# Moving table work between engines and overlapping the stages ahead of an attention loop

## The chip, the cores and the metric

The kernel runs on one NeuronCore of a Trainium2 chip. The metric is the device time of one execution in microseconds (us). A profile of one execution is used beside it; its span runs from the first to the last instruction of the program. TensorE does matmuls, VectorE and GpSimd elementwise work, ScalarE functions and copies, and DMA queues are fed by SP (SyncE), ScalarE and GpSimd.

## What is computed

Two independent halves are laid side by side in the output, [2048, 576 + 576].

```python
# A: sliding-window attention, 32 heads of 18 channels, window 256
qkv = x @ wqkv                                  # x [2048, 576]
p = softmax(where(0 <= i - j < 256, q @ k.T * 18 ** -0.5, -1e9))
a = (p @ v) @ wo
# B: diagonal state-space model, 576 channels, 128 states
dt = exp(log_dt)
P[d, n, l] = exp(dt[d] * (A_re + 1j * A_im)[d, n] * l)      # l = 0..2047
K[d, l] = real(sum_n C[d, n] * P[d, n, l] * dt[d] * B[d, n])
y = causal_convolution(u, K) + u * Dskip        # in the reference by an FFT over 4096
```

## The kernel before, in words

**Order of the work.** Everything up to the attention is written with pools of tiles and left to a scheduler, which fixes each engine's order when the kernel is built, from the order in which operations are emitted (`merge` interleaves several generators by weight) and its own estimates. From `attention` on the order is the written one (`manual_schedule`). Engines run their queues strictly in order. A pool gives a tile of a name one of a few buffers; a new tile waits until the old one's readers are done. Pools are stacked: memory of a closed pool is reused by pools opened later, whose first use waits for it.

**Projections (`proj`, L182 to L252).** x and the weights are scaled by a power of two from their largest absolute value (`amax`, L161; across partitions on GpSimd, L144) and split into a high and a low half-precision part: `wh`, `wl` (L209, L210), `xh`, `xl` (L226 to L229). So x is read twice: once in 8 slices of 256 columns for its maximum (L188 to L195), once for the split. Projections are 14 matmuls each (`mm14`, L172); their results are split again (L236, L237) and stored to DRAM as `qd` and `vd`.

**Tables (`s4_prep`, `tables`).** K is built from tables of exponentials and sines in 36 steps of 16 channels (`n = 2 * NQ`; two steps share one group q of 32). Angles come from small outer products on TensorE into PSUM (`outer`, L314, pool `xps`, two buffers). `fraction` (L318) rounds them on ScalarE (L324), subtracts on VectorE (L325) and takes the absolute value on ScalarE (L326). `exps_ab` and `exps_q` (L334, L344) are exponentials, for four steps at a time. `factors` (L348 to L371) takes two sines and then six operations on VectorE (L358, L364, L365, L367, L368, L369) to make `A` and `tr`. `products` (L380) multiplies these out on GpSimd into two tiles of a pool `P` with two buffers; `qtable` makes the other operand `Q` (sines L395, L396 into PSUM; L400 to L403 on VectorE); `taps` (L418) contracts both on TensorE, 64 matmuls a step, and every second step copies the result into the tile K (L424). ScalarE loads a new function table (ACT_TABLE_LOAD) whenever exponentials and sines alternate.

**First transform (`s1`, L454).** The convolution is a two-step transform. The first step is a matmul with `w1` (L461), an eviction (`evac`, L125: three of four on ScalarE, L128, the fourth on VectorE, L130) and a store to DRAM (`gx` for u, `gk` for K). For u it runs in 16 pieces beside the tables (`s1_u`); for K (`s1_k`) in 8 pieces of 1152 columns, after all pools of projections and tables are closed.

**Attention (`attention`).** `att_setup` clears the tiles for Q and K on VectorE (L596 to L599). Per unit (four heads, half of the sequence; 16 units) `load_unit` reads Q, K, V; `gmax` finds row maxima (matmul L636, VectorE L643) and writes them as a row into Q by a DMA; `scores` (L677, exponential L679, masks on GpSimd L688) and `values` (L700) follow in 96 items. The convolution's second step and inverse (`conv`, L480: L500, L508, L526 to L537) is cut into parts that are dealt to the items; six parts run beside `gmax(0)` before the first item. The output projection (L903) comes last.

The way in which the pools of the stages follow each other is this (`build`):

```python
with ExitStack() as ek:
    self.pool(ek, "K", 1)
    with ExitStack() as e1:
        ...
        with ExitStack() as e2:
            self.pool(e2, "prep", 1)
            self.s4_prep()
        for n, b in (("wq", 1), ("raw", 2), ("x", 1), ...):
            self.pool(e1, n, b)
        ...
        merge((proj, 56), (tables, 400), (s1u, 12))
    with ExitStack() as e1:
        ...                       # s1_k
with ExitStack() as e1:
    ...                           # attention
```

Of the kernel before, what the change touches and what calls it, by code (L numbers as in the profile page):

```python
# [102 lines left out]
class Kernel:  # L103
# [17 lines left out]
    def pool(self, es, name, bufs, space=None):  # L121
        kw = {} if space is None else {"space": space}
        self.p[name] = es.enter_context(self.tc.tile_pool(name=name, bufs=bufs, **kw))
# [37 lines left out]
    def amax(self, out, v):  # L161
        self.nc.vector.tensor_reduce(out, v, axis=AX.XY, op=OP.max, apply_absolute_value=True)
# [19 lines left out]
    def proj(self):  # L182
# [3 lines left out]
        amx = sp.tile([128, 12], F32, name="amx")  # L186
        wr = self.p["K"].tile([128, 5, 1728], F32, name="K")
        for c in range(8):  # L188
            t = self.p["raw"].tile([128, 5, 256], F32, name="raw")
            self.load_rows(t, a["xT"], slice(c * 256, c * 256 + 256))  # L190
            self.amax(amx[:, c:c + 1], t)
            if c % 2 == 0:
                cs = slice(c // 2 * 432, c // 2 * 432 + 432)
                self.load_rows(wr[:, :, cs], a["wqkv"], cs)
            yield  # L195
        for c in range(4):
            self.amax(amx[:, 8 + c:9 + c], wr[:, :, c * 432:c * 432 + 432])
            yield
        px, self.sx = self.pow2_scale(amx[:, 0:8], "x")
        pw, self.sw = self.pow2_scale(amx[:, 8:12], "w")  # L200
# [117 lines left out]
    def fraction(self, x, pool, n, w):  # L318
# [7 lines left out]
        nc.scalar.activation(ab, f, AF.Abs)  # L326
        return f, ab

    def exps_ab(self, s):

        for q in (2 * s, 2 * s + 1):
            x = self.outer(self.al, q, [self.mul["c_ca"]], 0, GC)
            m = self.p["mab"].tile([128, GC, 12], F32, name="mab")
            self.nc.scalar.activation(m, x.rearrange("p (c m) -> p c m", m=12), AF.Exp)  # L334
# [3 lines left out]
    def exps_q(self, s):  # L338

        for c in range(4 * s, 4 * s + 4):  # L340
            mg = self.p["mg"].tile([128, HC, 64], F32, name="mg")
            for e in range(2):
                x = self.outer(self.al, c // 2, [self.mul["c_cm"]], c % 2 * HC + e * 8, 8)
                self.nc.scalar.activation(mg[:, e * 8:e * 8 + 8], x.rearrange("p (c m) -> p c m", m=64), AF.Exp)  # L344
                yield
            self.mg[c] = mg

    def factors(self, q):  # L348

        nc, tt, pool = self.nc, self.nc.vector.tensor_tensor, self.p["ab"]  # L350
# [5 lines left out]
        nc.scalar.activation(tr[:, :, 1, :], v(f), AF.Sin, scale=TWO_PI)  # L356
        nc.scalar.activation(tr[:, :, 0, :], v(ab), AF.Sin, scale=-TWO_PI, bias=self.halfpi)
# [11 lines left out]
        nc.vector.scalar_tensor_tensor(A[:, :, 0:4], t2[:, :, 0], -1.0, t1[:, :, 1], op0=OP.mult, op1=OP.subtract)  # L369
# [19 lines left out]
    def qtable(self, c):  # L389
# [5 lines left out]
        nc.scalar.activation(sn, v(f), AF.Sin, scale=-TWO_PI)  # L395
# [627 lines left out]
```

## Time and profile before

| | us |
|---|---|
| median of 3 runs | 1079.5 (1076.2 to 1081.78) |
| the profiled execution | 1075.61 |
| its span | 1073.6 |

The profile's views are told where they are used. Rows of groups give the line, engine, operation, output and input tiles with their shapes, the count, then busy time in us and the mean of one in ns, then the engine's idle time just before them and who ended it. "PE" is TensorE's matmuls, "PEld" its weight loads, "DVE" VectorE, "ACT" ScalarE, "POOL" GpSimd, "SPq" SP's queue of DMAs. PEclk is the share of TensorE's full clock that was granted. A row of waits reads: engine and line that waited, who released it, us in total, times, longest. Busy time of TensorE contains stalls inside its pipeline.

### The profile page before, as it was taken

What the parts mean: (1) busy time and instruction counts of PE and PEld (TensorE: products, weight loads), DVE (VectorE), ACT (ScalarE), POOL (GpSimd) and SP (SyncE); (2) the same over time, 40 slices, a digit from 0 to 9 for tenths busy, and PEclk for the clock granted to TensorE, in tenths of its full rate; (3) what the DMA queues carried; (4) which work ended last, traced back from release to release, by engine and by line L of the source; (5) the groups of instructions that cost most, each with busy time, mean ns of one, the idle gap of its engine ahead of it and who ended that gap; (6) DMA issues with size and microseconds to landing.
All of it is one profiled execution on the core that took longest, in us unless ns stands there. A gap on an engine that the chain in (4) does not pass through costs nothing.

```text
span 1073.6 us, 26801 instructions
## 1 busy us (share of the span) xinstructions
PE 857.8 (80%) x10332; PEld 450.7 (42%) x10332; DVE 736.2 (69%) x1859; ACT 619.9 (58%) x955; POOL 511.1 (48%) x606
## 2 busy tenths in 40 slices
PE   1535879897988797987578888878888899988787
PEld 0313436554744464553234333333333344434345
DVE  2879685669576845226676788888878766767564
ACT  1776758776797784233146655566566656644471
POOL 0004344435452632010235677766876666666770
PEclk9966989998998998999889999999999999999999
DMA  9665423442344232588616456454645644579763
GB/s 271 168 184 160 105 53 88 109 94 59 85 111 96 55 74 64 130 217 239 188 49 180 138 147 175 147 148 127 176 113 177 185 118 142 146 185 256 204 190 121
DMA packets 155911, 152.27 MB, mean 142 GB/s; under 512 B 36856, under 2 KB 134392, under 8 KB 155592
## 3 DMA queue, kind: packets, MB, share of 16 engines
q1 hardware_dynamic: 148152, 131.98, 45.3%
q0 software_dynamic: 6128, 14.60, 5.4%
q10 hardware_dynamic: 1504, 3.99, 1.3%
q8 instruction: 81, 1.33, 0.6%
q14 instruction: 46, 0.38, 0.1%
HBM read 89.12 MB, written 61.01 MB: 140 GB/s over the span
## 4 chain that ended last, share of the span: by engine, by line
PE 37%; DVE 25%; ACT 10%; DMA 10%; issue 9%; POOL 5%; SPq 2%; DVEq 0%; ACTq 0%; POOLq 0%
PE pp L172 8%; PE r L636 4%; PE po L700 4%; PE r L903 4%; PE r L500 4%; PE kp L418 4%; PE pp L461 3%; DVE jk L643 3%; POOL P L688 2%; DMA gk<-g 2%; PE ST L677 2%; PE x L314 2%; PE r L508 2%; DVE tr L358 2%; ACT P L679 2%
## 5 line engine op out<-in xcount | busy, mean ns | idle before, releaser
L643 DVE CUSTOM_DVE_ANT_0 jk<-r,bias 128x288 f32<-128x288 f32 (+7 forms) x512 | 198.0, 433 | 88.7 <-PE r L636 88.0
L679 ACT ACTIVATE P<-ST,esc 128x1024 f32<-128x1024 f32 (+1 forms) x192 | 202.0, 1059 | 92.9 <-PE ST L677 92.1
L380 POOL TENSOR_TENSOR m<-A,tr 128x1024 f32<-128x1024 f32 x72 | 149.5, 2098 | 194.2 <-PE kp L418 139.1
L688 POOL TENSOR_SCALAR_AFFINE_SELECT P<-P 128x512 f32<-128x512 f32 x240 | 171.7, 745 | 103.2 <-ACT P L679 100.8
L636 PE MATMUL r<-K,qb 128*64 128x288 f16 (+7 forms) x1024 | 130.5, 297 | 36.7 <-DVE qb L627 10.7
L700 PE MATMUL po<-P,V 128*32 128x256 f32 (+2 forms) x1408 | 100.2, 395 | 17.5 <-POOL P L688 8.1
L418 PE MATMUL kp<-Q,m 128*32 128x64 f32 x4608 | 88.3, 230 | 27.6 <-DVE Q L401 10.0
L636 PEld LDWEIGHTS <-qb 128*64 128x64 f16 x1024 | 60.3, 109 | 119.3 <-issue 65.6
L536 POOL TENSOR_TENSOR Y<-t,t 64x288 f32<-64x288 f32 x64 | 53.5, 835 | 109.8 <-DVE t L531 107.8
L418 PEld LDWEIGHTS kp<-Q,m 128*32 128x32 f32 x4608 | 75.2, 116 | 56.3 <-issue 41.7
L461 PE MATMUL pp<-ut,w 128*128 128x288 f32 x128 | 52.8, 538 | 40.9 <-DMA ut<-in_u_dram 18.6
L677 PE MATMUL ST<-Q,K 64*128 64x384 f16 (+2 forms) x704 | 73.5, 280 | 3.0 <-DMA Q<-mt 2.9
L237 DVE SCALAR_TENSOR_TENSOR qst<-pp,qst 128x512 f16<-128x512 f32 x36 | 24.7, 685 | 64.7 <-ACT qst L236 61.8
L128 ACT ACTIVATE g<-pp 128x288 f32<-128x288 f32 (+1 forms) x84 | 34.5, 447 | 40.4 <-DMA gk<-g 22.0
L700 PEld LDWEIGHTS po<-P,V 128*32 128x32 f32 x1408 | 35.7, 110 | 52.5 <-issue 25.7
L537 POOL TENSOR_TENSOR Y<-t,t 64x288 f32<-64x288 f32 x64 | 54.5, 852 | 3.8
L461 PEld LDWEIGHTS pp<-ut,w 128*128 128x128 f32 x128 | 28.9, 245 | 61.1 <-issue 24.1
L326 ACT ACTIVATE ab<-k 128x512 f32<-128x512 f32 (+1 forms) x54 | 31.9, 590 | 37.0 <-DVE k L325 36.6
L172 PE MATMUL pp<-xh,wh 128*128 128x512 f16 x180 | 47.9, 388 | 1.2 <-DVE xh L229 1.2
L172 PEld LDWEIGHTS <-wh 128*128 128x128 f16 x324 | 32.0, 101 | 39.3 <-issue 6.6
L172 PE MATMUL pp<-xh,wl 128*128 128x512 f16 x180 | 48.3, 392 | 0.0
L500 PE MATMUL r<-tx,w 128*64 128x288 f32 x256 | 40.2, 430 | 9.9 <-DMA tx<-gx 8.7
(177 smaller groups left out, 1756.1 us busy)
## 6 DMA issues: line engine op xcount, KB each, us to landing
gx<-g SPq DMA_DIRECT2D x32, 288.0 KB
qd<-qst SPq DMA_DIRECT2D x72, 128.0 KB
gk<-g SPq DMA_DIRECT2D x16, 576.0 KB
tx<-gx SPq DMA_DIRECT2D x16, 576.0 KB
tk<-gk SPq DMA_DIRECT2D x16, 576.0 KB
h<-ho SPq DMA_DIRECT2D x16, 576.0 KB
raw<-in_xT_dram SPq DMA_DIRECT2D x16, 512.0 KB
Q<-qd SPq DMA_DIRECT2D x32, 216.0 KB
```

The source lines that it names most:

```text
L172: self.nc.tensor.matmul(ps, u, v, start=(i == 0), stop=(i == len(ops) - 1))
L380: self.nc.gpsimd.tensor_tensor(m, A[:, ch, a0:a0 + 8].unsqueeze(3).to_broadcast(sh), tr[:, ch, part, 0:8].unsqueeze(2).to_broadcast(sh), o ...
L418: nc.tensor.matmul(kp[32 * st:32 * st + 32, c % 2 * JJ2 + j, :], m[:, ch, a0:a0 + 32], Q[:, ch, term % 2, :], start=(term == 0), stop=(ter ...
L461: nc.tensor.matmul(ps, self.w1[:, part, :], src[:, o:o + k], start=True, stop=True)
L500: nc.tensor.matmul(ps[64 * par:64 * par + 64], w2[:, par, 64 * part:64 * part + 64], t[:, 2 * hs:2 * hs + 2, par, :], start=True, stop=True)
L537: nc.gpsimd.tensor_tensor(Y[par][64:128], t1[sl, 1], t2[sl, 1], op=OP.add)
L636: nc.tensor.matmul(ps[64 * b:64 * b + 64, :n], self.qb[:, b, t, :], d["K"][:, b, k0:k0 + n], start=True, stop=True, skip_group_check=True)
L643: nc.vector.tensor_tensor_reduce(out=jk[:, :n], in0=ps[:, :n], in1=self.bias[:, 288 - n:], scale=1.0, scalar=-3e38, op0=OP.add, op1=OP.max ...
L677: nc.tensor.matmul(ps[:, u, o:o + n], d["K"][h, jp, k0:k0 + 128], d["Q"][h, jp, q0:q0 + n], start=True, stop=True, skip_group_check=True)
L679: nc.scalar.activation(pt[:, 2 * jp:2 * jp + 2, lo:hi], ps[:, :, lo:hi], AF.Exp, scale=self.esc)
L688: nc.gpsimd.affine_select(v, v, pattern=[[0, 4], [sg, 128]], compare_op=OP.is_ge, fill=0.0, base=-1 if far else 0, channel_multiplier=-sg)
L700: nc.tensor.matmul(self.po[32 * j:32 * j + 32, t0 * 128:t1 * 128], V[:, kb * 76 + 19 * j:kb * 76 + 19 * j + 32], pt[:, j, o:o + (t1 - t0) ...
```

## The change

1. **x is read first.** `proj` reads x once, contiguously, in five pieces into the buffers that later hold `wh`, `wl` and one `qst`, takes its maxima, and then reads the weights; its first step is emitted ahead of `s4_prep`. x is still read a second time for the split.
2. **Two-sided pools.** Pools get a side of the memory and finer waits for reuse: projections, K, the first transform and their loads lie on the right, tables and then the attention on the left. So buffers for x don't wait for `prep`, and attention's tiles not for the projections' pools.
3. **Absolute values masked.** The sign bit is cleared on VectorE instead of the absolute value on ScalarE.
4. **Table factors on GpSimd.** The six operations of `factors` move from VectorE to GpSimd (the last becomes a multiplication of `A[8:12]` by -1). `products(c + 1)` is emitted after `taps(c - 1)`.
5. **Ordered functions.** Exponentials and sines go through `act`, which makes the scheduler keep their written order on ScalarE. By the built order ScalarE loads a table 19 times instead of 37.
6. **K's transform.** 16 pieces of 576 columns instead of 8 of 1152, with the PSUM buffers of the projections; ten run after the tables, six beside `gmax(0)`, where six parts of the convolution ran. Those are dealt to the items (101 parts instead of 95 over the same 76 items). The weights of `merge` now let tables, projections and u's transform end together.

```diff
     def pool(self, es, name, bufs, space=None, side="left"):
         kw = {} if space is None else {"space": space}
+        if space != DRAM:
+            kw.update(side=side, reuse_waits="tile")
...
-        for c in range(8):
-            t = self.p["raw"].tile([128, 5, 256], F32, name="raw")
-            self.load_rows(t, a["xT"], slice(c * 256, c * 256 + 256))
-            self.amax(amx[:, c:c + 1], t)
...
+        flat = a["xT"].rearrange("r c -> (r c)").rearrange("(p n) -> p n", p=128)
+        for i, nm in enumerate(("wh", "wl")):
+            t = wp.tile([128, 4320], F32, name=nm)
+            for c in range(2):
+                o = 2160 * (2 * i + c)
+                nc.sync.dma_start(t[:, 2160 * c:2160 * c + 2160], flat[:, o:o + 2160])
+                self.amax(amx[:, 2 * i + c:2 * i + c + 1], t[:, 2160 * c:2160 * c + 2160])
+        t = self.p["pst"].tile([128, 576], F32, name="qst")
+        nc.sync.dma_start(t, flat[:, 8640:])
+        self.amax(amx[:, 4:5], t)
         for c in range(4):
-            self.amax(amx[:, 8 + c:9 + c], wr[:, :, c * 432:c * 432 + 432])
-            yield
+            cs = slice(c * 432, c * 432 + 432)
+            self.load_rows(wr[:, :, cs], a["wqkv"], cs)
+            self.amax(amx[:, 5 + c:6 + c], wr[:, :, cs])
+        yield
...
-        nc.scalar.activation(ab, f, AF.Abs)
+        nc.vector.tensor_scalar(ab.bitcast(I32), k, 0x7FFFFFFF, None, op0=OP.bitwise_and)
         return f, ab
+
+    def act(self, *args, **kw):
+
+        self.tc.stamp_issue_order_token(self.nc.scalar.activation(*args, **kw).ins, "transcendentals")
...
     def factors(self, q):
 
-        nc, tt, pool = self.nc, self.nc.vector.tensor_tensor, self.p["ab"]
+        nc, tt, pool = self.nc, self.nc.gpsimd.tensor_tensor, self.p["ab"]
...
-        nc.vector.scalar_tensor_tensor(A[:, :, 0:4], t2[:, :, 0], -1.0, t1[:, :, 1], op0=OP.mult, op1=OP.subtract)
+        nc.gpsimd.tensor_scalar(A[:, :, 0:4], A[:, :, 8:12], -1.0, None, op0=OP.mult)
...
             if c + 1 < n:
-                self.products(c + 1)
                 self.phases(c + 1)
                 yield
...
             if c:
                 yield from self.taps(c - 1)
+            if c + 1 < n:
+                self.products(c + 1)
...
-        for b in range(8):
-            self.s1(kf[:, b * 1152:(b + 1) * 1152], self.gk, 8 * b, 8, "s1p")
+        for b in range(16):
+            self.s1(kf[:, b * 576:(b + 1) * 576], self.gk, 4 * b, 4, pp[0])
...
-                k = share(n - 2, 95, 76) if n < 78 else share(n - 78, 16, 17) if n < 95 else 0
+                k = share(n - 2, 101, 76) if n < 78 else share(n - 78, 16, 17) if n < 95 else 0
...
+            self.pool(ek, "K", 1, side="right")
+            self.pool(ek, "s1s", 2, side="right")
+            self.pool(ek, "pps", 3, PSUM, side="right")
...
+                for n, b in (("s1u", 2), ("wq", 1), ("raw", 2), ("x", 1), ("pst", 2)):
+                    self.pool(e1, n, b, side="right")
...
+                next(proj)
                 with ExitStack() as e2:
                     self.pool(e2, "prep", 1)
                     self.s4_prep()
...
+                merge((part(proj, 4), 4), (part(tables, 16), 16), (part(s1u, 2), 2))
+                merge((proj, 56), (tables, 308), (s1u, 14))
+                for _ in part(s1k, 10):
+                    pass
...
+                self.attention_start()
+                merge((self.gmax(0), 19), (s1k, 6))
+                self.begin(1)
+                ek.close()
```

`attention_start` loads units 0 and 1, as the head of `attention` did. The exponential tables get four buffers (`mab`) instead of three.

More of the change, by code (lines that the diff above doesn't have):

```diff
@@ L515, in conv @@
         nx = load(0)
+        yield
         last = None
@@ L780, in attention @@
             self.begin(n)
+            if n == 0:
+                next(conv)
             streams = []
@@ L980, in build @@
                 nc.sync.dma_start(self.dsk, a["dsk"].partition_broadcast(128))
[L981 to L987 removed]
+                self.attention(self.conv())
+            e0.close()
 def kernel(**inputs):
```

83 lines of the change are left out of this document (35 added, 48 removed).

## The prediction

> **What bounds the kernel now.** I read the page's head first, then the busy time by stage, then what TensorE waits for in the longest stage.
>
> ```profile
> span 1073.6 us, 26801 instructions
> PE 857.8 (80%) x10332; PEld 450.7 (42%) x10332; DVE 736.2 (69%) x1859; ACT 619.9 (58%) x955; POOL 511.1 (48%) x606
> ```
> ```profile
> core 0: us, PE busy (x) PEld busy (x) DVE busy (x) ACT busy (x) POOL busy (x), PEclk, DMA share, GB/s
> 0.00:101.60 101.60, 38.91 (x321) 21.22 (x322) 69.81 (x79) 56.98 (x71) 11.23 (x13) 0.82 0.70 199
> 101.60:421.00 319.40, 269.75 (x5281) 165.47 (x5280) 221.95 (x328) 237.52 (x405) 141.09 (x68) 0.93 0.36 85
> 421.00:466.00 45.00, 44.90 (x251) 25.57 (x249) 7.12 (x11) 10.28 (x22) 1.45 (x4) 1.00 0.59 129
> 466.00:513.00 47.00, 35.69 (x97) 17.63 (x96) 26.73 (x26) 16.20 (x36) 3.51 (x1) 0.96 0.84 240
> 513.00:543.50 30.50, 16.09 (x109) 7.76 (x110) 20.29 (x80) 5.44 (x11) 6.93 (x10) 0.81 0.50 147
> 543.50:1073.60 530.10, 452.50 (x4278) 213.02 (x4277) 390.31 (x1336) 293.52 (x412) 346.89 (x510) 0.98 0.56 158
> ```
>
> The stretches are mine. Up to 101.6 us no projection runs: inputs land, maxima are taken. From 101.6 to 421 projections (L172) and tables (L418) share TensorE; to 466 the rest of the projections runs alone; to 513 the transform of the kernel K (L461 on K) runs alone, with the DMA at 0.84 of its time; to 543.5 the first maxima (L636, L643) and six parts of the convolution; then attention, 530.1 us, which the change hardly touches. So the change has 543.5 us to work on. In the mixed stretch TensorE is busy 269.75 of 319.4 us, at a granted clock of 0.93 against 1.00 where projections run alone. What it waits for there:
>
> ```profile
> PE x L314 <- DVE k L325: 19.3, 5, 6.1
> PE pp L461 <- DVE qst L237: 9.1, 2, 4.9
> PE kp L418 <- ACT K L424: 5.1, 6, 1.4
> PE kp L418 <- POOL m L380: 4.3, 3, 2.5
> PE kp L418 <- DVE Q L401: 4.3, 1, 4.3
> PE kp L418 <- issue: 3.6, 3, 1.5
> ```
>
> Eight waits on VectorE make 32.7 us, among them the long ones; GpSimd makes 4.3. The bound is TensorE, broken by a VectorE that falls behind, with ScalarE (237.5 of 319.4) close behind it.
>
> **The change part by part.**
>
> *1. Start.* Rows, from the timeline, the chain and the page:
>
> ```profile
> 50.20 0.16 DVE L143 TENSOR_REDUCE wm<-amx 128x1 f32<-128x4 f32 x1
> 56.17 2.12 ACT L265 ACTIVATE ps<-res 32x2304 bf16<-32x2304 f32 x1
> 58.31 0.39 SPq L135 DMA_DIRECT2D raw<-in_xT_dram  x1
> 101.57 2.98 PE L172 MATMUL pp<-xh,wh 128*128 128x512 f16 x12
> ```
> ```profile
> 95.40 0.39 POOL xg L144
> ```
> ```profile
> GB/s 271 168 184 160 105 53 88 109 94 59 85 111 96 55 74 64 130 217 239 188 49 180 138 147 175 147 148 127 176 113 177 185 118 142 146 185 256 204 190 121
> q10 hardware_dynamic: 1504, 3.99, 1.3%
> ```
>
> Weights' maximum is known at 50.2, but x is first read at 58.31, as the preparation's last instruction (56.17 + 2.12) frees the memory that its buffers take; x's maximum comes at 95.4, the first projection at 101.57. Afterwards x stands first in SP's queue: 4.72 MB, then 4.42 MB of weights (one slab twice), beside ScalarE's queue of 3.99 MB: 13.1 MB. At the first slice's 271 GB/s that is 48 us, at the first stretch's 199 it is 66. From maximum to projection were 6.2 us; four weight splits may make it 12. First projection at 54 to 78; I take 65, in the middle: **37 us earlier**.
>
> *2. Mixed stretch.* What leaves VectorE, and what leaves ScalarE:
>
> ```profile
> L358 DVE TENSOR_TENSOR tr<-tr,mab 128x768 f32<-128x768 f32 x18 | 25.5, 1418 | 7.3 <-ACT tr L357 6.9
> L364 DVE TENSOR_TENSOR t<-tr,wr 128x256 f32<-128x256 f32 x18 | 20.4, 1132 | 0.4
> L365 DVE TENSOR_TENSOR t<-tr,wi 128x256 f32<-128x256 f32 x18 | 16.3, 904 | 0.0
> L367 DVE TENSOR_TENSOR A<-t,t 128x128 f32<-128x128 f32 x18 | 7.9, 439 | 0.3
> L369 DVE SCALAR_TENSOR_TENSOR A<-t,t 128x128 f32<-128x128 f32 x18 | 6.8, 379 | 0.0
> L368 DVE TENSOR_TENSOR A<-t,t 128x128 f32<-128x128 f32 x18 | 6.8, 379 | 0.0
> L325 DVE TENSOR_TENSOR k<-x,k 128x512 f32<-128x512 f32 x36 | 24.5, 681 | 1.6 <-ACT k L324 1.3
> ```
> ```profile
> L326 ACT ACTIVATE ab<-k 128x512 f32<-128x512 f32 (+1 forms) x54 | 31.9, 590 | 37.0 <-DVE k L325 36.6
> L395 ACT ACT_TABLE_LOAD x10 | 12.8, 1283 | 0.2
> ```
>
> VectorE loses 25.5 + 20.4 + 16.3 + 7.9 + 6.8 + 6.8 = 83.7 us. It gains 54 mask operations, not in this trace: not below nothing, not above an operation of the same size with two inputs (0.68 us, L325), so 0 to 37 us; I take 0.45, or 24, near the upper row, as the size is the same. ScalarE loses 54 absolute values, 31.9 us, and 18 table loads: the built order has 37 before and 19 after, 18 x 1.283 = 23.1 us. Both then have idle time that hides what they gain; without that cover the masks' 24 us would lengthen the chain from fraction to sine. With VectorE's waits gone, the copies of K (5.1) and GpSimd's products (4.3) are late next.
>
> GpSimd takes the factors. Rows for its speed:
>
> ```profile
> L380 POOL TENSOR_TENSOR m<-A,tr x72: 1947/1957/2939, 80.1 to 407.6; 128x1024 f32<-128x1024 f32 x72
> L358 DVE TENSOR_TENSOR tr<-tr,mab x18: 937/1072/2707, 76.9 to 395.0; 128x768 f32<-128x768 f32 x18
> ```
> ```profile
> L380 POOL TENSOR_TENSOR m<-A,tr 128x1024 f32<-128x1024 f32 x72 | 149.5, 2098 | 194.2 <-PE kp L418 139.1
> L536 POOL TENSOR_TENSOR Y<-t,t 64x288 f32<-64x288 f32 x64 | 53.5, 835 | 109.8 <-DVE t L531 107.8
> ```
>
> A line through 288 elements in 835 ns and 1024 in 1957 gives 1.57 us for 768, 0.79 for 256, 0.59 for 128: per group of 32 channels 1.57 + 2 x 0.79 + 3 x 0.59 = 4.9 us (at worst six of 2.94: 17.6; below 4.9 only by a fixed cost smaller than the line's). With four products, 7.8, it is 12.7 us for each of 18 groups. Its queue has a wait ahead of them: in the built order two pairs of products stand before each group's factors, and a pair waits until the taps two steps back have freed its buffer (139 us of such idle time today cost nothing). Whoever waits for those factors comes a group later, 19 us of slack against 12.7 of work.
>
> The Trainium skill ("GPSIMD Engine Reference", Engine selection) speaks against this move: two-input elementwise work belongs on VectorE, GpSimd being about twice as slow. By it a group's factors would take about 5.2 us, twice the 2.6 of VectorE's shortest rows, and the sum would stay, as a group of the forecast lasts 19 us.
>
> TensorE then needs: busy 269.75 + 44.90 = 314.7 us, plus what no longer fits ahead of the first projection (by the built order 10 of 21 matmuls on u, 4 of 22 outer products and 128 taps, so some 15 of the first stretch's 38.9 us), less the lost clock: 0.07 of 319.4 is 22 us; I take 14 back, as some gaps stay. Idle was 49.8. Of the 32.7 on VectorE I take 25 away, since the operations that swell (L358 from 0.94 to 2.71) are those that leave; GpSimd's 4.3 (and the waits of weight loads on it) I raise by 8. Sum: 314.7 + 15 - 14 + 49.8 - 25 + 8 = 348, so projections and tables, now merged to end together, end at **413** instead of 466. All VectorE waits gone and full clock, from 54: 54 + 307.7 + 17.1 = 379; nothing won and GpSimd's waits four times as long, from 78: 78 + 329.7 + 49.8 + 13 = 470.
>
> *3. K's transform.*
>
> ```profile
> gk<-g SPq DMA_DIRECT2D x16, 576.0 KB
> L461 PE MATMUL pp<-K,w 128*128 128x384 f32 x96 | 35.6, 517 | 11.1 <-ACT g L128 9.5 <-ACT vst L248 1.6
> ACT g L128 <- DMA gk<-g: 19.7, 10, 3.7
> ```
>
> Its stores, 9.4 MB, filled the 47 us at 240 GB/s; evictions waited 19.7 us for them. Afterwards 10 of 16 pieces come first: 5.9 MB and 1.7 MB of Q and K for two units, whose loads stand among the first of these stores in SP's queue and wait behind them, at 240 GB/s 32 us, of which TensorE's 10/16 x 35.6 = 22 is hidden. VectorE's clearing of Q and K stays beside it, as now. The other six pieces go beside the first maxima instead of six parts of the convolution: TensorE 13 us for 6/16 of 35.6, and the maxima's own about 9 (16.09 less the convolution's 7), so 22 to 26 with the stores hidden. With the mask rows sent to Q: 32 + 24 + 2 = **58** against 77.5. Ends: 48 (TensorE alone) and 70.
>
> *4. Attention.* The six parts are now done inside the items:
>
> ```profile
> L500 PE MATMUL r<-tx,w 128*64 128x288 f32 x256 | 40.2, 430 | 9.9 <-DMA tx<-gx 8.7
> ```
> ```profile
> 535.87 1.21 PE r L508 x4
> ```
>
> Six parts are two units, each of 16 instructions on L500 (two lines like this one, 40.2 / 256 = 0.157 us each) and four on L508 (1.21): 3.7 us, 7.4 together, in a stretch where TensorE is busy 452.5 of 530.1: 0 to 8, I take 5.
>
> *Sum:* 413 + 58 + 530 + 5 = 1006, and 2.0 outside the span (the profiled execution took 1075.61): **1008 us**, against 1079.5 for the median, 0.4% above the profiled one.
>
> **Rivals.**
>
> *Everything opens up:* ScalarE, at 237.5 - 31.9 - 23.1 = 182 of 348, and VectorE never hold TensorE; the mixed stretch ends at 379 to 390: 974 to 985. For it: the five long waits all name VectorE. Against: such gaps seldom all close when order is fixed ahead.
>
> *The waits change owner:* ScalarE now takes exponentials and sines strictly in the written order, ten exponentials at a time, with the next sines queued behind them; TensorE waits for tables as it did for VectorE. Then 65 + 329.7 + 49.8 = 445 and the time 1040. For it: 36 table steps at 9 us is what this stretch does now. The rule behind it in the Trainium skill ("SBUF — State Buffer", Who interferes with whom) is that a VectorE operation in a two-port mode, as masking may be, and a GpSimd operation exclude each other for a whole instruction. L358's 0.94 to 2.71 us agrees; for masks no run here shows it. As mechanism of this kernel: 54 masks each held for one product of 1.96 us add 106 us to VectorE, which at 222 - 84 + 24 + 106 = 268 of 348 gets late again: same 1040.
>
> *GpSimd becomes the bound,* the slower side. A group must take it more than (348 + 71) / 18 = 23.3 us for the time to pass 1079.5; 12.7 is forecast, and ten operations at the longest recorded 2.94 make 29.4. At 25 us a group: 65 + 450 + 10 = 525, and 1120. It decides from factors of 15.5 us instead of 4.9 on. Against: 72 products have a median of 1957 ns, ten above the shortest.
>
> *The transform gains nothing:* two 288 KB stores in flight instead of two of 576 leave the fixed part of a store uncovered: 77 instead of 58, 1027.
>
> **How the numbers follow.** Forecast 0.60 (985 to 1027), everything opens up 0.13, waits change owner 0.16, transform gains nothing 0.05, GpSimd the bound 0.06. Time 1008; range 970 to 1050: it leaves out GpSimd's case and the outer ends of the first two rivals, some 0.12. A measurement here tells about 0.5%, 5.4 us: faster 0.93, same 0.02, slower 0.05.
>
> **What would show it.** First projection near 65, last near 413; PE clock over 0.95 in between; waits of L314's line on VectorE gone, those on GpSimd's products near 12 us; 19 table loads; factors near 4.9 us a group; first scores 58 us after the last projection. A GpSimd busy over 0.9 in the mixed stretch, or TensorE idle there over 50 us, would make the forecast wrong.

## The result, and the profile after

| | before | forecast | after |
|---|---|---|---|
| median of the runs, us | 1080.64 (4 runs) | 1008 | 1044.46 (4 runs, 1042.13 to 1046.75) |
| first projection at | 101.6 | 65 | 83.5 |
| from there until tables and projections are done | 364.5 | 348 | 340.0 |
| from there to the first scores | 77.4 | 58 | 68.7 |
| from there to the end | 530.1 | 535 | 548.2 |

The changed kernel takes 0.9679 of the time before (95% interval 0.9658 to 0.9701). It is some 36 us faster where 71.5 were forecast: sign and range held, the size was twice too large. The stretches are those of the profiled execution (span 1040.4 us). They miss by 18.5, -8, 10.7 and 13 us, 34 in all: 10.5 until tables and projections are done, the rest in the transform and the attention.

The head of the page after, and the busy time by stage (columns as in the prediction):

```profile
span 1040.4 us, 26877 instructions
PE 840.5 (81%) x10364; PEld 448.8 (43%) x10364; DVE 710.3 (68%) x1806; ACT 572.3 (55%) x895; POOL 585.5 (56%) x714
```
```profile
0.00:83.50 83.50, 18.20 (x40) 9.10 (x41) 55.62 (x48) 39.67 (x41) 3.55 (x9) 0.98 0.72 211
83.50:423.50 340.00, 308.52 (x5812) 191.31 (x5810) 219.21 (x318) 215.94 (x385) 233.00 (x187) 0.98 0.45 104
423.50:466.30 42.80, 31.44 (x91) 18.23 (x92) 24.02 (x24) 13.33 (x33) 0.00 (x0) 0.84 0.65 194
466.30:492.20 25.90, 19.30 (x105) 11.47 (x105) 15.46 (x74) 7.85 (x17) 0.00 (x0) 0.93 0.47 138
492.20:1040.40 548.20, 463.09 (x4322) 218.72 (x4321) 395.96 (x1344) 295.48 (x420) 348.91 (x518) 0.97 0.55 158
```

The second row is the forecast's stretch: TensorE busy 308.5 of 340, GpSimd 233 instead of 143, ScalarE and VectorE with room. The third and fourth are the transform; in the third the DMA moves 194 GB/s, not 240. What TensorE waits for in the second row:

```profile
PE x L320 <- DVE k L331: 7.3, 5, 5.9
PE kp L428 <- issue: 5.2, 5, 1.7
PE pp L174 <- DVE xh L235: 5.2, 2, 4.0
PE pp L472 <- DVE qst L243: 4.8, 3, 2.4
PE pp L472 <- ACT g L130: 3.8, 3, 2.4
PE kp L428 <- POOL m L390: 2.4, 2, 2.2
```

The long line of before (19.3 us behind VectorE's fractions) is 7.3, of which 5.9 are one wait behind a split of x on VectorE, and GpSimd's products cost 2.4. GpSimd's groups, and the masks:

```profile
L390 POOL TENSOR_TENSOR m<-A,tr 128x1024 f32<-128x1024 f32 x72 | 145.7, 2046 | 88.4 <-PE kp L428 88.4
L368 POOL TENSOR_TENSOR tr<-tr,mab 128x768 f32<-128x768 f32 x18 | 33.0, 1833 | 38.0 <-ACT tr L337 37.8
L375 POOL TENSOR_TENSOR t<-tr,wi 128x256 f32<-128x256 f32 x18 | 12.3, 683 | 0.0
L374 POOL TENSOR_TENSOR t<-tr,wr 128x256 f32<-128x256 f32 x18 | 11.4, 634 | 1.3
L379 POOL TENSOR_SCALAR A<-A 128x128 f32<-128x128 f32 x18 | 10.5, 581 | 1.5
L377 POOL TENSOR_TENSOR A<-t,t 128x128 f32<-128x128 f32 x18 | 8.8, 488 | 1.3
L378 POOL TENSOR_TENSOR A<-t,t 128x128 f32<-128x128 f32 x18 | 8.4, 465 | 0.0
```
```profile
L332 DVE TENSOR_SCALAR ab<-k x54: 342/572/2171, 83.4 to 413.9; 128x512 int32<-128x512 int32 x36, 128x384 int32<-128x384 int32 x18
```

The six factor rows add up to 84.4 us, 4.7 a group (forecast 4.9). A mask (duration: shortest, median, longest in ns) takes 0.35 to 0.41 us or up to 2.17.

### The profile page after: what moved, and what is told of

It is laid out like the page before. It is cut to its first block, busy times and chain, and to the rows that moved or that the text cites. A ratio compares the mean times of both kernels' runs of the same rounds, so it can differ in the third digit from the quotient of the medians.

```text
span 1040.4 us, 26877 instructions
## 1 busy us (share of the span) xinstructions
PE 840.5 (81%) x10364; PEld 448.8 (43%) x10364; DVE 710.3 (68%) x1806; ACT 572.3 (55%) x895; POOL 585.5 (56%) x714
## 4 chain that ended last, share of the span: by engine, by line
PE 41%; DVE 21%; DMA 13%; issue 9%; ACT 7%; POOL 4%; SPq 3%; DVEq 0%; ACTq 0%; POOLq 0%
PE pp L174 9%; PE r L648 5%; PE po L712 5%; PE r L918 4%; PE pp L472 3%; PE kp L428 3%; PE r L511 3%; PE r L519 3%; PE ST L689 3%; DVE jk L655 2%; PE x L320 2%; DMA c_ca<-in_c_ca_dram 2%; DVE qb L639 2%; DMA gk<-g 2%; DMA K<-in_wqkv_dram 2%
## 5 line engine op out<-in xcount | busy, mean ns | idle before, releaser
L700 POOL TENSOR_SCALAR_AFFINE_SELECT P<-P 128x512 f32<-128x512 f32 x240 | 167.7, 727 | 162.1 <-ACT P L691 159.6
L390 POOL TENSOR_TENSOR m<-A,tr 128x1024 f32<-128x1024 f32 x72 | 145.7, 2046 | 88.4 <-PE kp L428 88.4
L472 PE MATMUL pp<-ut,w 128*128 128x288 f32 x128 | 44.3, 476 | 61.2 <-DMA ut<-in_u_dram 46.7
L428 PE MATMUL kp<-Q,m 128*32 128x64 f32 x4608 | 77.3, 220 | 7.8 <-issue 5.2
L428 PEld LDWEIGHTS kp<-Q,m 128*32 128x32 f32 x4608 | 67.8, 110 | 29.5 <-issue 23.3
L130 ACT ACTIVATE g<-pp 128x288 f32<-128x288 f32 x96 | 36.9, 411 | 50.5 <-DMA gk<-g 24.9
L472 PEld LDWEIGHTS pp<-ut,w 128*128 128x128 f32 x128 | 25.5, 215 | 74.1 <-issue 46.9
L368 POOL TENSOR_TENSOR tr<-tr,mab 128x768 f32<-128x768 f32 x18 | 33.0, 1833 | 38.0 <-ACT tr L337 37.8
L331 DVE TENSOR_TENSOR k<-x,k 128x512 f32<-128x512 f32 (+1 forms) x54 | 34.0, 639 | 29.7 <-ACT k L330 29.2
L243 DVE SCALAR_TENSOR_TENSOR qst<-pp,qst 128x512 f16<-128x512 f32 x36 | 24.6, 684 | 42.8 <-ACT qst L242 29.1
L472 PE MATMUL pp<-K,w 128*128 128x288 f32 x128 | 44.0, 488 | 11.4 <-ACT g L130 10.0
```

The costliest lines, as they stand in the source:

```text
L390: self.nc.gpsimd.tensor_tensor(m, A[:, ch, a0:a0 + 8].unsqueeze(3).to_broadcast(sh), tr[:, ch, part, 0:8].unsqueeze(2).to_broadcast(sh), o ...
L428: nc.tensor.matmul(kp[32 * st:32 * st + 32, c % 2 * JJ2 + j, :], m[:, ch, a0:a0 + 32], Q[:, ch, term % 2, :], start=(term == 0), stop=(ter ...
L472: nc.tensor.matmul(ps, self.w1[:, part, :], src[:, o:o + k], start=True, stop=True)
L700: nc.gpsimd.affine_select(v, v, pattern=[[0, 4], [sg, 128]], compare_op=OP.is_ge, fill=0.0, base=-1 if far else 0, channel_multiplier=-sg)
```

## The experiments

All ratios are to the kernel before, run on the same chip, with 95% intervals; the changed kernel's is 0.968. Theory: the factors' move gives the gain, and the rest of the forecast was lost in three places: queues in strict order delay the first projection; two small store buffers slow the transform; and the convolution's parts are dearer among the attention's items than forecast. Rivals are with each run.

**Where the gain comes from.** The kernel before with the factors' move alone (`p_factors`):

```diff
-        nc, tt, pool = self.nc, self.nc.vector.tensor_tensor, self.p["ab"]
+        nc, tt, pool = self.nc, self.nc.gpsimd.tensor_tensor, self.p["ab"]
...
+        nc.gpsimd.tensor_scalar(A[:, :, 0:4], A[:, :, 8:12], -1.0, None, op0=OP.mult)
```

> The kernel before, with only the factors moved to GpSimd. If VectorE with the factors in its queue is what holds TensorE, its waits on VectorE's lines (33 us there) fall below 15, its clock between the first and the last projection rises over 0.96 from 0.94, and the time falls by 15 to 35 us, to 1043 to 1063. If the move only makes room for the masks that the change adds, the time stays within 6 us of the kernel before. If factors behind products on GpSimd come too late, it rises.

Measured: 1044.08 us, 0.9671 (0.9649 to 0.9694). This one edit is worth as much as the whole change: beside it the change's transform is 10 us shorter (68.7 instead of 78.7) and its attention 11 longer (548.2 instead of 537.4). The first stages of `p_factors`, and all that outer products wait there for VectorE's fractions:

```profile
0.00:108.20 108.20, 43.38 (x452) 24.42 (x453) 69.77 (x73) 65.51 (x84) 23.21 (x27) 0.82 0.66 187
108.20:429.40 321.20, 300.28 (x5399) 183.37 (x5398) 156.98 (x236) 237.97 (x413) 202.28 (x166) 0.99 0.44 102
```
```profile
PE x L314 <- DVE k L325: 0.6, 2, 0.4
```

19.3 us of waits became 0.6, and the clock 0.99. What stood ahead of the fractions can be read in the kernel before. The longest of the five waits, and three of the ten operations that VectorE runs without a break from 147.24 to 155.37 us:

```profile
147.24 2.58 DVE L358 TENSOR_TENSOR tr<-tr,mab 128x768 f32<-128x768 f32 x1 [0.98 <-ACT tr L357]
149.85 2.06 DVE L364 TENSOR_TENSOR t<-tr,wr 128x256 f32<-128x256 f32 x1
154.69 0.68 DVE L325 TENSOR_TENSOR k<-x,k 128x512 f32<-128x512 f32 x1
155.42 0.48 PE L314 MATMUL x<-c_ca,al 96*128 96x384 bf16 x1 [6.11 <-DVE k L325]
```

All six factors of a group, 5.9 us together, stand ahead of the subtraction (L325) that sets an angle tile free. Four of the five waits are of this kind, with 4.4 to 7.2 us of factors ahead.

The reverse, from the changed kernel: `b_factors` puts the two lines back, `b_abs` only the absolute values, `b_both` both.

```diff
-        nc.vector.tensor_scalar(ab.bitcast(I32), k, 0x7FFFFFFF, None, op0=OP.bitwise_and)
+        nc.scalar.activation(ab, f, AF.Abs)
```

> The seven operations of a group's factors go back from GpSimd to VectorE (with the negation as a two-input operation again). If the move frees TensorE of waits on VectorE as the prediction's term of 25 us has it, TensorE's waits on VectorE's fractions go from 7 back to about 15 to 20 us in the stretch and the time rises by 8 to 15 us, to 1052 to 1060. If VectorE had room anyway (219 us busy of 340), or GpSimd's slower factors cost as much as they free, the time stays within 4 us.

> The absolute values go back from VectorE's mask to ScalarE's Abs, behind the subtraction. If the longer chain through ScalarE (copy, subtraction on VectorE, absolute value on ScalarE again: 27 us of ScalarE's idle time in the kernel before stood in front of it) is part of what the change gained, the dense stretch grows by 5 to 12 us. If ScalarE has room (216 us busy of 340), it stays within 3 us and the time within 3 of 1044.

> Factors back on VectorE and absolute values back on ScalarE, so that the dense stretch has the engines of the kernel before, with one order for exponentials and sines, the products behind the taps and x read first. Factors on VectorE with the masks there too gave a stretch of 382 us. If the move of the factors only makes room for the masks, the stretch comes back to 340 to 350 and the time to 1042 to 1052. If VectorE is too full for the factors with or without the masks (it would be busy some 235 of 340 us), it stays at 360 to 380 and the time at 1062 to 1078.

Measured: `b_factors` 1079.71 us, 1.0027 (1.0007 to 1.0048): all of the gain is gone, more than I expected. `b_abs` 1041.23, 0.9659 (0.9634 to 0.9684): not to be told from the changed kernel; ScalarE had room. `b_both` 1073.31, 0.9963 (0.9935 to 0.9992): the factors are what VectorE can't take, with or without masks. The dense stretches of `b_factors` and `b_both`, and the wait of TensorE behind fractions in `b_both`:

```profile
83.60:465.80 382.20, 330.24 (x5812) 201.92 (x5810) 276.69 (x427) 216.02 (x385) 152.74 (x79) 0.92 0.39 93
```
```profile
82.00:456.60 374.60, 323.40 (x5812) 199.99 (x5810) 244.71 (x372) 241.87 (x438) 151.56 (x79) 0.95 0.41 97
```
```profile
PE x L320 <- DVE k L331: 20.0, 8, 4.1
```

VectorE is busy only 245 of 375 us there, and still TensorE waits 20 us for its fractions: the next outer product needs one of the two PSUM tiles of angles, and both are taken until VectorE's queue has come to their subtractions. In five of these eight waits (9 of the 20 us) factors stand in VectorE's queue ahead of them, in the other three products for `Q` or a split of x. The share of busy time did not show this; the waits did. Whether TensorE loses more by the factors' own work or by their waits for GpSimd (below) isn't told apart by these runs.

`b_order` issues exponentials and sines without a common order.

```diff
-        self.tc.stamp_issue_order_token(self.nc.scalar.activation(*args, **kw).ins, "transcendentals")
+        self.nc.scalar.activation(*args, **kw)
```

> The exponentials and sines are issued without the common order between them, so that ScalarE loads its table of functions some 40 times instead of 19, at 1283 ns each: some 27 us more on ScalarE. If loads stand in front of what TensorE waits for, the dense stretch grows by 8 to 20 us and the time goes to 1052 to 1064. If ScalarE's idle time (124 us of 340 in the stretch) takes them in, the time stays within 3 us.

Measured: 1051.63 us, 0.9764 (0.9737 to 0.9791); the stretch is 348 us. By the ratios the order is worth some 9 us. ScalarE loads its tables 43 times instead of 19 there, but TensorE's idle time in the stretch is the same (31.3 us); its busy time is what grew, by 8 us, and how the order brings that is not shown.

**The start.** `x_old` takes the maxima as before. `a_start1` issues the first five steps of the projection ahead of all first exponentials, `a_start2` ahead of the parameter arithmetic too; `a_start3` is `a_start2` with tables and projections dealt as in the changed kernel. `a_start2`'s edit is this one; in `a_start1` the two added lines stand behind the preparation, in `a_start3` the projection waits one turn in the second `merge`. `x_old` has the loop that the diff of the change takes out.

```diff
                 next(proj)
+                for _ in part(proj, 5):
+                    pass
                 with ExitStack() as e2:
...
-                merge((part(proj, 4), 4), (part(tables, 16), 16), (part(s1u, 2), 2))
-                merge((proj, 56), (tables, 308), (s1u, 14))
+                merge((part(tables, 16), 16), (part(s1u, 2), 2))
+                merge((proj, 55), (tables, 308), (s1u, 14))
```

> The maxima are taken as in the kernel before (eight blocks of x through the two raw buffers, weights between them, then the four weight maxima); all else is the changed kernel. If the first projection's start sets the end of the dense stretch, as the prediction's sum has it, the first product comes near 100 us and the time rises by 14 to 20 us, to 1058 to 1065. If the tables set that end (their products start at 92.8 us and take 331 us in the changed kernel, 90.2 and 330 in the kernel before), the first projection comes later by the same 15 to 20 us, the last table product stays within 4 us of 423.5, and the time rises by less than 6.

> The projection's five scaling steps (four of wh and wl, the first block of xh and xl) are issued ahead of all sixteen first exponentials instead of between them. If the order of ScalarE's queue holds the first projection back (25 us from the maxima at 58 to the first product at 83.5), the first product comes at 70 to 74 us and the time falls by 6 to 12 us, to 1033 to 1039. If the exponentials and tables behind them bind the stretch, the first product moves but the last one does not: the time stays within 3 us of 1044.

> The same five steps and the two scales are issued ahead of the parameter arithmetic of the tables as well. If the order of the queues of ScalarE and VectorE is the cause, the maxima are reduced as soon as the last weights are read (about 50 us, not 58), the first product comes at 62 to 68 us and the time falls by 10 to 18 us, to 1027 to 1035. If the tables bind, their first factors come some 8 us later than now and the gain is given back: 1040 to 1048. If landing of x and the weights binds, the first product does not come ahead of 75.

> As a_start2 (scales and the first block of x and weights ahead of the tables' parameter arithmetic), but the projection's parts fall between the tables' parts at the same places as in the changed kernel (one step later than in a_start2). If a_start2 lost its ten microseconds to another interleaving, with TensorE idle for over 5 us in each group of tables and its clock down after it, the dense stretch keeps the 340 us of the changed kernel and the time falls to 1033 to 1037. If the tables' own begin sets the end (first product 96.5 there, 92.8 in the changed kernel), the last table product comes at 427 to 434 again and the time is 1044 to 1050.

Measured: `x_old` 1050.05 us, 0.9753 (0.9723 to 0.9784); `a_start1` 1050.54, 0.9743 (0.9712 to 0.9774); `a_start2` 1049.56, 0.9737 (0.9707 to 0.9767); `a_start3` 1045.1, 0.9695 (0.9668 to 0.9722). The queues do delay the first projection: in `a_start2` it comes at 73.6 us. But no time is won (`a_start1` and `a_start2` lose some 6 us, which neither of their expectations had), so my theory of the start fell as a cause of time. The stages up to and after the first projection of `x_old` (first part only), `a_start2` and `a_start3` say why:

```profile
0.00:90.80 90.80, 21.40 (x43) 9.40 (x44) 58.61 (x53) 42.30 (x45) 5.04 (x10) 1.00 0.72 194
```
```profile
0.00:73.60 73.60, 9.22 (x18) 5.13 (x19) 51.75 (x41) 29.72 (x22) 5.42 (x9) 0.92 0.78 236
73.60:433.50 359.90, 325.08 (x5833) 199.03 (x5831) 223.67 (x324) 225.34 (x403) 232.82 (x187) 0.95 0.42 100
```
```profile
0.00:76.90 76.90, 12.26 (x27) 7.46 (x28) 54.96 (x46) 33.32 (x27) 5.42 (x9) 0.89 0.77 235
76.90:430.30 353.40, 317.17 (x5825) 195.24 (x5823) 219.11 (x319) 222.85 (x398) 233.25 (x187) 0.96 0.43 101
```

Length less busy time of TensorE in the first stretch is its idle time: 62.7 us before, 65.3 after, 64.4 and 64.6 in `a_start2` and `a_start3`, 64.8 in `p_factors`, 69.4 in `x_old` and in `a_start1`. An earlier projection only changes places with the work on u and the angles that stood ahead of it (busy 18.2 falls to 9.2). What is late in the changed kernel is TensorE's first work of all; and the maxima, known at 58 us, are followed by 25 us until the first projection:

```profile
46.69 4.18 PE L472 MATMUL pp<-ut,w 128*128 128x288 f32 x8 [46.69 <-DMA ut<-in_u_dram]
54.44 0.82 PE L320 MATMUL x<-c_ca,al 96*128 96x384 bf16 x2 [3.57 <-ACT al L271]
```
```profile
58.15 0.14 DVE L145 TENSOR_REDUCE wm<-amx 128x1 f32<-128x4 f32 x1
```

u lands behind x and the weights at 46.7 us; from there to 83.5 TensorE idles 18.6 us more. In the kernel before u came first and TensorE's work began at 16.1 us, but its gaps up to the first projection sum to nearly the same, for which the runs show no reason. Loading u or the angles' operands first was not tried.

**K's transform.** `k_buf` gives the second half of each of the first ten pieces two further store buffers; `k_late` loads the second unit behind the first maxima; `k_serial` emits all pieces ahead of the maxima. The diff shows their edits in the order `k_buf`, `k_serial`, `k_late`.

```diff
-            st = self.p["s1s"].tile([128, n], F32, name="g1")
+            if g is self.gk and part and l0 < 40:
+                st = self.p["raw"].tile([128, 5, 256], F32, name="raw").rearrange("p a b -> p (a b)")[:, 0:n]
+            else:
+                st = self.p["s1s"].tile([128, n], F32, name="g1")
...
-                for _ in part(s1k, 10):
+                for _ in s1k:
...
-        self.load_unit(1)
...
+                self.load_unit(1)
                 self.begin(1)
```

> In the first ten pieces of the kernel's transform the second half goes out of two more store buffers (the free tiles of the input's raw blocks), so that four are in turn and not two. If the two buffers bind the stage (ScalarE's evictions wait 24 us for stores in it), the stretch from the last table to the first scores shrinks from 42.8 to 33 to 37 us and the time by 5 to 9. If the transfers themselves bind, or the queue that issues them behind the loads of the first heads, the stretch stays within 2 us.

> The loads of the second unit of heads are issued behind the last piece of the transform and the first maxima, not ahead of them. If the stage is slow because its stores stand on SP's queue behind loads that wait for memsets on VectorE, the first pieces run at the 3.2 us of the later ones and the stretch from the last table to the first scores shrinks from 68.7 to 60 to 64 us. If the two store buffers alone bind it, it stays within 2 us. If the second unit's maxima then wait for its loads, the attention grows by up to 6 us and takes the gain back.

> All sixteen pieces of the kernel's transform are done ahead of the first maxima; none stand beside them. The stretch from the last table to the first scores is 68.7 us in the changed kernel, of which the last six pieces and the maxima take 25.9 together. If running the two side by side gains what the prediction has it gain, the six pieces come out again at 3 to 4 us each and the maxima at 20 as in the kernel before: 83 to 88 us, and the time rises by 14 to 18, to 1058 to 1063. If the two only share TensorE and the stores, the stretch grows by less than 6 us.

Measured: `k_buf` 1042.12 us, 0.9660 (0.9623 to 0.9696), the stretch from the last table to the first scores 62.6 us instead of 68.7 (the 42.8 of the expectation is its first part, to 466.3 us): buffers bind it, but the attention behind it is 5 us longer and the time isn't told apart. `k_late` 1046.48, 0.9713 (0.9683 to 0.9742): the stretch 69.5, TensorE then waits 9.4 us for the loads of the first scores. `k_serial` 1042.71, 0.9682 (0.9650 to 0.9715), is inconclusive: its stretch is 61.4 us, but the scheduler dealt the last pieces among the maxima by itself (the last at 485.5 us).

**The attention.** `c_conv15` leaves out one frequency pair; `c_first6` opens the attention's pools behind the whole transform and runs six parts beside the first maxima, as before; `best2` is that with four store buffers for all pieces, `best1` with absolute values on ScalarE as well. The first pair of lines is `c_conv15`'s, the second that of the other three, the last all four's.

```diff
-        for fp in range(16):
+        for fp in range(15):
...
-                merge((self.gmax(0), 19), (s1k, 6))
+                merge((self.gmax(0), 19), (part(conv, 7), 7))
...
-                k = share(n - 2, 101, 76) if n < 78 else share(n - 78, 16, 17) if n < 95 else 0
+                k = share(n - 2, 95, 76) if n < 78 else share(n - 78, 16, 17) if n < 95 else 0
```

> The last of the sixteen frequency pairs of the convolution is left out (the store of the fifteenth is written twice), and 95 parts are spread over the attention instead of 101, as in the kernel before. If the six parts that moved into the attention cost what TensorE spends on them there (its busy time grew by 10.6 us), the time falls by 9 to 14 us, to 1031 to 1036. If their price is near the 5 us of the prediction and the rest of the loss is a collision (the wait for the output weights at 676 us) or a later begin of the convolution, it falls by 2 to 6 us.

> The changed kernel with all sixteen pieces of the transform ahead of the first maxima, the attention's pools opened at once behind them, and six parts of the convolution beside the first maxima again, 95 in the items, as in the kernel before. If the six parts cost little beside the first maxima, where TensorE waits for VectorE and for loads, the stretch from the last table to the first scores is 61 to 66 us, the attention 530 to 533 and the time 1022 to 1028. If the parts cost their 16 us at either place, or the first of them waits for the last stores and loads of the convolution, the stretch is 74 to 80 us and the time stays at 1038 to 1045.

> c_first6 with two more store buffers in the transform and the absolute values on ScalarE. If both still bring what they did by themselves (6 us of the stretch and 3 us), the time is 4 to 9 us below that of c_first6. If the begin of the attention is bound by loads of the convolution or of the heads, or VectorE's masks cost nothing, it stays within 3 us of it.

> c_first6 with two more store buffers in the transform alone (masks on VectorE). If store buffers bind the transform, the stretch from the last table to the first scores falls by 4 to 7 us and the time by as much below c_first6. If what comes behind waits for the same transfers, it stays within 2 us.

Measured: `c_conv15` 1030.27 us, 0.9555 (0.9523 to 0.9587). Its attention is the 530 us of before again:

```profile
492.50:1024.30 531.80, 453.70 (x4282) 212.92 (x4281) 392.03 (x1336) 293.13 (x412) 345.80 (x510) 0.98 0.57 160
```

Against the changed kernel's last row six parts cost 16.4 us of the attention: 9.4 of TensorE's busy time and 7.0 of idle time around it (by the medians, 14 us of the time). `c_first6` 1052.19, 0.9743 (0.9718 to 0.9769); `best2` 1030.22, 0.9552 (0.9527 to 0.9577); `best1` 1030.34, 0.9544 (0.9523 to 0.9565). `c_first6` is slower than the changed kernel, outside both of its expectations, and the other two are 22 us below it, more than I expected. The attentions of `c_first6` and `best2` are short again (530.6 and 528.9 us), but in `c_first6` the transform, from the last table to its last store's issue, is far longer than in `best2`. The stretch, and ScalarE's wait for the stores up to the last piece's matmul 2 us before its end, in `c_first6`, then in `best2` (there over both kinds of buffers):

```profile
427.00:491.80 64.80, 42.87 (x136) 25.29 (x136) 26.50 (x37) 18.59 (x49) 0.00 (x0) 0.91 0.58 169
```
```profile
ACT g L130 <- DMA gk<-g: 41.3, 29, 4.4
```
```profile
427.00:472.70 45.70, 39.39 (x136) 23.03 (x136) 26.50 (x37) 18.84 (x48) 0.00 (x0) 0.97 0.87 245
```
```profile
ACT raw L130 <- DMA gk<-raw: 5.7, 7, 1.2
...
ACT g L130 <- DMA gk<-g: 3.9, 6, 1.0
```

The same 136 matmuls, at 169 and at 245 GB/s of all DMA: with two stores of 288 KB in flight the DMA engines are busy 0.58 of the time, with four 0.87.

**Two more.** `best3` is `best1` with tables dealt as before, so that they end some 45 us ahead of the projections; `best4` moves the products ahead of the angles again, too.

```diff
-                merge((proj, 56), (tables, 308), (s1u, 14))
+                merge((proj, 56), (tables, 400), (s1u, 12))
```

> best1 with the tables dealt as in the kernel before (400 and 12 parts against 56 of the projection, not 308 and 14), so that they end some 40 us ahead of the projections, which then run alone. If ending together costs TensorE waits that a tail of projections alone does not have (with the factors' move alone it idles 21 us of the stretch and 32 in the changed kernel), the last projection comes at 405 to 414 instead of 422 and the time falls to 1014 to 1023. If TensorE is short of work only at the start (about 65 us idle in every run so far), the last projection stays at 418 to 426 and the time at 1026 to 1034.

> best3 with the products emitted ahead of the next step's angles again, as in the kernel before and in the run with the factors' move alone. If the place behind the taps makes the factors late, the time falls by another 3 to 8 us below best3. If GpSimd has room at either place (233 us busy of 340), it stays within 3 us of best3; if factors now stand behind products that wait for their buffer, it rises by 3 to 10.

Measured: `best3` 1028.03 us, 0.9535 (0.9510 to 0.9559); `best4` 1028.48, 0.9528 (0.9495 to 0.9561). Neither differs from `best1` by more than the intervals; the last projection comes at 415.7 (between the two expectations) and 418.6 instead of the 421.6 of the last table in `best1`. The place of the products doesn't matter. With `best1` and `best2` these are the fastest versions that leave nothing out: nearly 5% below the kernel before, and some 15 us below the changed kernel.

## Why the prediction was half right

By TensorE alone, in us, until tables and projections are done:

| | end | idle up to the first projection | idle from there | busy |
|---|---|---|---|---|
| before | 466.1 | 62.7 | 49.8 | 353.7 |
| forecast | 413 | 41.1 | 32.8 | 339.6 |
| after | 423.5 | 65.3 | 31.5 | 326.7 |
| the factors' move alone | 429.4 | 64.8 | 20.9 | 343.7 |

**1. Start: wrong.** "First projection at 54 to 78; I take 65 ... 37 us earlier" followed x from its landing to the first projection. The landing was right (maxima at 58 us, 48 to 66 forecast); the 6 to 12 us from the maxima to the first projection were 25. That alone is not the loss, since `a_start2` took 10 us of it away and won no time. I did subtract the matmuls that no longer fit ahead of it, but took for granted that the 41 us left would be all the idle time. TensorE has no work before 46.7 us and idled 62 to 70 us up to the first projection in every run, whatever came first. The step that failed is using the first projection's time as the start of TensorE's work; its term was worth 21.6 us of idle time and gave none. `x_old` is 0.7% slower, but so are `a_start1` and `a_start2`, which read x first: that reading x first is worth something by itself isn't shown.

**2. Mixed stretch: right in mechanism, and too small.** Idle time came out at 31.5 where 32.8 was forecast, in part by luck: TensorE's waits on VectorE fell from 35 to 17.5 us, less than the 25 taken away, and those on GpSimd's products to 2.4 instead of rising by 8. Busy time fell by 27 us where 14 less were taken for the clock (of the same 5852 matmuls). The clock was the larger part of these 27: in the kernel before each of TensorE's seven longest gaps between first and last projection (2.5 to 6.1 us) comes with 3.4 or 6.8 us at half the clock, begun inside the gap or within 1 us behind it, and with the gaps these go too (in the changed kernel, where the gaps of 4.0 and 5.9 us have them and those of up to 2.4 don't, the longest begins at 336.0 and the half clock at 339.1). Half of TensorE's busy time at half clock is 23 us before and 6 after, an estimate from the traces' clock records: 17 of the 27. The other 10 stay open. `p_factors` and `b_factors` show the cause: factors off VectorE. Of the other edits in this stretch the order of functions is worth 0.9%, the masks nothing. GpSimd did not become the bound: it is busy 0.69 of the stretch. Of "the waits change owner" ScalarE's half did not come.

VectorE's half did in part. By the trace's start and end times, 34 of the 54 masks last over 10% longer than an undisturbed one; each runs beside GpSimd operations, for 0.9 to 1.3 times as long as it overlaps them. One of them, and the GpSimd operations beside it:

```profile
130.97 2.15 DVE L332 TENSOR_SCALAR ab<-k 128x512 int32<-128x512 int32 x1
```
```profile
130.88 4.05 POOL L390 TENSOR_TENSOR m<-A,tr 128x1024 f32<-128x1024 f32 x2
```

The two products take 4.05 us together, and the mask, 0.41 us when alone, ends 0.3 us behind the first of them. Masks sum to 47.6 us; undisturbed (0.35 us for the 18 smaller, 0.41 for the 36 larger) they would take 21. That is some 26 us of waiting, not the 106 of the rival, and VectorE had room for it. The Trainium skill ("SBUF — State Buffer", Who interferes with whom) gives this as an exclusive lock on a shared port pair, held for the whole instruction; the trace agrees. It also says what made the factors so dear on VectorE, as it names operations with both inputs in SBUF, which the factors are: the six rows of before sum to 83.7 us, and 18 times their shortest durations to 46.4, so 37 us of them were such waiting (factors that ran beside no GpSimd operation stayed within 0.03 us of the shortest). The rule that I weighed against the move ("GPSIMD Engine Reference", Engine selection: two-input work is about twice as slow there) holds per instruction, 1833 ns against VectorE's shortest 937, and decides nothing here: GpSimd had room and VectorE's queue was what TensorE waited for.

**3. K's transform: one term mis-sized.** "At 240 GB/s 32 us" took the rate of stores of 576 KB for stores of half the size in as many buffers. The DMA reached 194 GB/s, and the first part took 42.8 us instead of 32; the six pieces beside the maxima, with 25.9 us, came out as forecast (24 and 2). That is the mechanism of my rival "the transform gains nothing" (0.05), at part of its price: 68.7 instead of 58 or 77. With four buffers 245 GB/s came back.

**4. Attention: one term mis-sized.** The six parts were priced at TensorE's 7.4 us and taken at 5 for a stretch that had idle time. They cost 16.4: 9.4 busy, and 7.0 idle. Each part also puts evictions and products on ScalarE's and VectorE's queues, and the maxima's matmuls wait for PSUM tiles `r` until these have read them. Two such waits in the attention of the changed kernel, then the same two in the kernel before:

```profile
PE r L648 <- DVE t L542: 11.5, 28, 0.6
...
PE r L648 <- ACT X L538: 4.4, 13, 0.8
```
```profile
PE r L636 <- DVE t L530: 7.7, 22, 0.4
...
PE r L636 <- ACT X L526: 2.4, 5, 0.8
```

Together they are 5.8 us longer after, beside the 7.0 of idle time. Beside the first maxima TensorE has idle time, and with four store buffers the whole is as fast there, in `best2` with all parts, as `c_conv15` without six. The place isn't free: the stretch from the last table to the first scores is 73.7 us in `best2` and 67.4 in `c_conv15`, with two buffers only; what buffers and place are worth each in `best2` isn't told apart.

What stays open: why moving only the factors leaves an attention of 537 us, 7 longer than before, with the same instructions (TensorE's busy time there is 5.5 us longer, at a granted clock of 0.97 instead of 0.98, in the slowest of its five runs); what would shorten the 65 us of idle time at the start; and why `a_start2` lets clock and gaps take back more than `a_start3`, beyond their different dealing.

## What to carry to other kernels

Account for a start by the idle time of the engine that binds, not by when one stage's first instruction runs: a stage that is moved ahead may only change places with other work. Look for the queue in which the binding engine's releaser stands, however idle the releaser's engine is on average; moving what stands ahead of it was worth as much as all else together here, even at twice the price per operation. Work that goes from a stretch with idle time into one that binds costs its busy time and the queueing that it brings to every engine it touches; and halving the size of stores without more buffers lowered their rate here.

## What the runs showed of the hardware

- VectorE's mask with input and output in SBUF lasts about as long as the GpSimd operation that runs beside it (342 ns to 2171); subtractions with an operand in PSUM do not change (L331 for 128x512 in the changed kernel: a mean of 684 ns wholly beside GpSimd operations, 685 beside none).
- With two stores of 288 KB in flight all DMA together moved 169 to 194 GB/s, with four 245, with two of 576 KB 240.
